# Attention, ELU and tanhshrink layers on one core: how the first pairs of heads are prepared, placed and scheduled, and the transpose of the last 64 keys

## Chip, cores and metric

The kernel runs on one core of a Trainium2 chip. The metric is the device time of one execution in microseconds (us). Engines are PE (TensorE; its weight loads are listed apart as PEld), DVE (VectorE), ACT (ScalarE), POOL (GpSimd) and SP (SyncE, which here only issues DMAs).

## What is computed

An attention with rotary position encoding over 4 batches x 8 heads, 576 positions, head size 64, all in float32; then two dense layers over the 2304 tokens. The change touches the attention alone. Cut to what matters:

```python
def _attn_ref(q, k, v):                       # (4, 8, 576, 64)
    def rotate(x):
        x1, x2 = x[..., :half], x[..., half:]
        return np.concatenate([x1 * cos - x2 * sin, x1 * sin + x2 * cos], axis=-1)
    q_rot, k_rot = rotate(q), rotate(k)
    scores = scale * np.matmul(q_rot, k_rot.transpose(0, 1, 3, 2))
    scores = scores - np.max(scores, axis=-1, keepdims=True)
    attn = np.exp(scores)
    attn = attn / (np.sum(attn, axis=-1, keepdims=True) + 1e-09)
    return np.matmul(attn, v)

def reference(...):
    x = attn_out.transpose(0, 2, 1, 3).reshape(2304, 512)
    x = elu(x @ moe_w_in) @ moe_w_out
    h = x @ moe2_w_in
    return (h - np.tanh(h)) @ moe2_w_out
```

## The kernel before

The 32 heads are worked in 16 pairs. A pair has nine items: four blocks of 128 queries (u = 0 to 3) for each of its two heads (h = 0, 1), and one item (u = 4, h = None) with the last 64 queries of both heads. So there are 144 items, and one loop over i runs them in an order written out by hand. In step i it emits, in this order: the loads that are due, the row maximum of item i on DVE (L224), the scores of item i+1 on PE (L215), the exponentials of item i on ACT (L238), the copies of the last step's transposes out of PSUM (L269 on DVE, L271 on ACT), the normalising of item i-1 on POOL (L255, with a sum and a reciprocal on DVE, L251 and L252), the preparation steps that are due, one part of a weight conversion, the transposes of item i-4 on PE (L295 and, for the last 64 keys, L308 or L301), and the products with v that are due on PE (L329). Each engine works its own instructions strictly in this order. Scores lie in two PSUM buffers, so the scores of item i+2 wait for the exponentials of item i.

**Preparation.** Before a pair can be scored, q and k of both heads (x = 0 and x = 1 in `prep`) pass five steps: multiply with the cosine table (step 0) and the sine table (step 1), add (step 2), round to a high part on ACT (step 3, L155), and take the low part on DVE (step 4, L160). Then `place` copies high and low parts by DMA to where the matmuls want them: four DMAs of 288 KB for k (L182) and four of 144 KB for q (L185). These read 64 partitions and write 64; the loads from memory (L130, L359, L361) write all 128. The first two items are scored directly from the sums of step 2 (L197), without the parts. For pair 1 the table `early` gives the step i at which each of the five is emitted: before the change (0, 0, 1, 2, 3) for q and (0, 0, 0, 1, 2) for k; its loads are issued right behind those of pair 0. The multiplications of step 0 of later pairs run on POOL, step 1 on DVE for pairs 0 and 1 and on POOL from pair 2 on.

**Weight conversion.** In the attention, eight blocks of the dense layers' weights are also converted (`conv_w`), each in five parts spread over every second step: part 0 on ACT (L74), part 1 two DVE instructions (L76, L77), parts 2 and 3 one each (L81, L85), part 4 ACT and POOL (L91, L92). With c = 9*(p%2) + r - 3 they fall, for an even pair, on the steps r = 3, 5, 7 of its nine and on r = 0 and 2 of the next pair.

**Last 64 keys.** Each transposed block of probabilities has 128 keys; 576 leaves 64. For the blocks u = 0 to 3 one 128x128 transpose serves both heads (L308). For u = 4 two 64x64 matmuls with the identity do it (L301), and the copy out is 128x64. The last product with v reads 64 rows of the one head and 64 rows of zeros.

## Time and profile before

| | |
|---|---|
| median of 3 runs | 1100.6 us (1100.6 to 1100.99) |
| the profiled execution | 1101.16 us, its span 1099.0 us |
| PE busy in the span | 1060.1 us (96%) |
| PEld, DVE, ACT, POOL busy | 960.0, 756.5, 724.3, 697.6 us |
| attention, up to the last product with v | about 311 us |
| first items, up to the transposes of item 8 | 45.6 us |
| first matmul of the kernel | 12.46 us, when the second sum of pair 0 is ready (12.41 us) |
| pair 1 on DVE | its additions done at 19.15 us, its low parts at 26.6 us |
| PE without work before item 8 | 32.3 to 34.1 us; its granted clock then 0.50, from 34.7 to 38.1 us |

The span runs from the first to the last instruction of the trace; the profiled execution's own time is 2.16 us longer. A busy PE is not a PE at its peak, so the table says only that PE is seldom without work, and where it is not.

### The profile page before, as it was taken

What the parts mean: (1) busy time and instruction counts of PE and PEld (TensorE: products, weight loads), DVE (VectorE), ACT (ScalarE), POOL (GpSimd) and SP (SyncE); (2) the same over time, 40 slices, a digit from 0 to 9 for tenths busy, and PEclk for the clock granted to TensorE, in tenths of its full rate; (3) what the DMA queues carried; (4) which work ended last, traced back from release to release, by engine and by line L of the source; (5) the groups of instructions that cost most, each with busy time, mean ns of one, the idle gap of its engine ahead of it and who ended that gap; (6) DMA issues with size and microseconds to landing.
All of it is one profiled execution on the core that took longest, in us unless ns stands there. A gap on an engine that the chain in (4) does not pass through costs nothing.

```text
span 1099.0 us, 18847 instructions
## 1 busy us (share of the span) xinstructions
PE 1060.1 (96%) x6512; PEld 960.0 (87%) x6512; DVE 756.5 (69%) x1435; ACT 724.3 (66%) x1562; POOL 697.6 (63%) x652
## 2 busy tenths in 40 slices
PE   2999999999999999999999999999999999999998
PEld 1777777777889999999999999988998999888986
DVE  6888889888745564675776765376767667766674
ACT  2676767777757666565555555488777877878672
POOL 3888888888558856555455565566566655755552
PEclk9999999999999999999999999999999999999999
DMA  7777676867214444354443673255445754456431
GB/s 232 215 214 190 187 199 200 215 186 206 74 45 139 125 157 141 101 178 152 127 144 128 225 240 117 94 211 194 167 158 197 252 205 163 181 163 231 169 127 58
DMA packets 85950, 184.27 MB, mean 168 GB/s; under 512 B 10592, under 2 KB 46432, under 8 KB 85856
## 3 DMA queue, kind: packets, MB, share of 16 engines
q1 hardware_dynamic: 78080, 154.76, 44.4%
q10 hardware_dynamic: 7776, 28.32, 8.8%
q8 instruction: 52, 0.85, 0.3%
q14 instruction: 42, 0.34, 0.1%
HBM read 126.94 MB, written 27.79 MB: 141 GB/s over the span
## 4 chain that ended last, share of the span: by engine, by line
PE 79%; DVE 9%; POOL 4%; ACT 3%; issue 2%; DMA 2%; SPq 0%; ACTq 0%; POOLq 0%; DVEq 0%
PE y L511 18%; PE h L454 18%; PE yb L705 14%; PE hb L740 9%; PE o L329 7%; PE s L215 6%; PE pt L295 4%; PE cvb L740 3%; DVE nm L224 2%; DVE fn L773 1%; DMA v<-in_v 1%; POOL blk L495 1%; DVE aT L269 1%; DVE t L152 1%; POOL blk L612 1%
## 5 line engine op out<-in xcount | busy, mean ns | idle before, releaser
L255 POOL TENSOR_SCALAR a<-a,r 128x576 f32<-128x576 f32 x144 | 137.0, 963 | 56.9 <-DVE r L252 37.7
L495 POOL TENSOR_TENSOR gt<-fn,gt 128x384 fp32r<-128x384 f32 x119 | 123.3, 1036 | 76.7 <-ACT gt L494 69.1
L238 ACT ACTIVATE a<-s,nm 128x576 f32<-128x576 f32 x144 | 107.2, 744 | 85.7 <-DVE nm L224 71.6
L705 PE MATMUL yb<-wb,blk 128*128 128x512 f32 x603 | 154.3, 392 | 0.4 <-POOL blk L495 0.4
L740 PE MATMUL hb<-blk,wa 128*128 128x384 f32 x720 | 139.8, 337 | 2.0 <-DVE fn L773 2.0
L740 PEld LDWEIGHTS hb<-blk,wa 128*128 128x128 f32 x720 | 127.0, 188 | 7.3 <-DVE fn L773 3.0
L705 PEld LDWEIGHTS yb<-wb,blk 128*128 128x128 f32 x603 | 112.5, 188 | 22.7 <-POOL blk L495 0.8
L462 ACT ACTIVATE fn<-h 128x384 f32<-128x384 f32 x96 | 47.3, 492 | 125.1 <-PE h L454 105.7
L224 DVE TENSOR_REDUCE nm<-s 128x1 f32<-128x576 f32 x144 | 107.8, 752 | 30.1 <-PE s L215 28.2
L495 POOL TENSOR_TENSOR blk<-fn,blk 128x384 fp32r<-128x384 f32 x67 | 71.3, 1064 | 87.9 <-ACT blk L494 59.4
L454 PE MATMUL h<-blk,wa 128*128 128x384 f32 x576 | 107.9, 335 | 0.8 <-POOL blk L55 0.6
L511 PE MATMUL y<-gt,wa 128*128 128x384 f32 x576 | 107.7, 334 | 0.1
L454 PE MATMUL h<-blk,wb 128*128 128x384 f32 x576 | 107.6, 334 | 0.0
L511 PE MATMUL y<-gt,wb 128*128 128x384 f32 x576 | 107.6, 334 | 0.0
L479 DVE TENSOR_SCALAR cvb<-fm 128x512 f32<-128x512 f32 x56 | 38.9, 694 | 98.9 <-ACT fm L477 96.3
L454 PEld LDWEIGHTS h<-blk,wa 128*128 128x128 f32 x576 | 100.3, 188 | 1.8 <-POOL blk L55 0.9
L511 PEld LDWEIGHTS y<-gt,wa 128*128 128x128 f32 x576 | 100.5, 188 | 0.4 <-issue 0.4
L511 PEld LDWEIGHTS y<-gt,wb 128*128 128x128 f32 x576 | 100.6, 188 | 0.0
L454 PEld LDWEIGHTS h<-blk,wb 128*128 128x128 f32 x576 | 100.5, 188 | 0.0
L92 POOL TENSOR_TENSOR fm<-fm,fn 128x512 fp32r<-128x512 f32 (+1 forms) x48 | 58.3, 1219 | 57.0 <-ACT fn L91 55.8
L150 POOL TENSOR_TENSOR t<-t,tabs 128x576 f32<-128x576 f32 x59 | 86.1, 1460 | 6.4 <-DMA t<-in_qk 6.3
L329 PE MATMUL o<-aT,v 128*64 128x256 f32 (+1 forms) x768 | 88.2, 336 | 1.9 <-ACT aT L271 1.8
(128 smaller groups left out, 2289.2 us busy)
## 6 DMA issues: line engine op xcount, KB each, us to landing
wa<-wi SPq DMA_DIRECT2D x96, 448.0 KB, 4.9
wb<-wo SPq DMA_DIRECT2D x48, 512.0 KB, 5.9
k<-hl SPq DMA_DIRECT2D x64, 288.0 KB, 4.7
t<-in_qk SPq DMA_DIRECT2D x30, 576.0 KB, 5.1
fm<-in_w2o ACTq DMA_DIRECT2D x16, 512.0 KB, 3.8
fm<-in_w2i ACTq DMA_DIRECT2D x14, 512.0 KB, 3.6
fm<-in_w1i ACTq DMA_DIRECT2D x12, 512.0 KB, 3.7
wi<-fn SPq DMA_DIRECT2D x24, 256.0 KB, 2.0
```

Source lines behind the costliest of these rows:

```text
L92: nc.gpsimd.tensor_tensor(out=lo, in0=f, in1=hi.bitcast(F32), op=ALU.subtract)
L150: eng.tensor_tensor(out=t[:, i, :], in0=t[:, i, :], in1=tabs[:, i, :], op=ALU.mult)
L215: nc.tensor.matmul(out=s[:, half, o0:o0 + n], lhsT=w, rhs=k[:, part, c0:c0 + n], start=(m == 0 and part == 0), stop=(m == len(terms) - 1 a ...
L224: nc.vector.tensor_reduce(out=nm, in_=s_t[i][:, :, 0:288], axis=AX.XY, op=ALU.max, negate=True)
L238: nc.scalar.activation(out=a.rearrange("p (x c) -> p x c", x=2), in_=s[:, :, 0:288], func=AF.Exp, bias=nm_t.pop(i), scale=1.0, accum_out=den,)
L255: nc.gpsimd.tensor_scalar(out=a, in0=a, scalar1=r[:, x:x + 1], scalar2=1.0, op0=ALU.mult, op1=ALU.mult)
L329: nc.tensor.matmul(out=o[sl, 0:n], lhsT=w, rhs=m, start=(c == 0), stop=(c == 4))
L454: nc.tensor.matmul(out=hp, lhsT=w[:, wp, ws], rhs=x_hl(t, xp, c), start=(m == 0), stop=(m == 3 * KC - 1))
L495: nc.gpsimd.tensor_tensor(out=g[:, 1, :], in0=f, in1=g[:, 0, :].bitcast(F32), op=ALU.subtract)
L511: nc.tensor.matmul(out=y_t[e][:, 0:NB], lhsT=w[:, wp, es], rhs=gt[:, gp, :], start=st, stop=sp)
L705: nc.tensor.matmul(out=y, lhsT=gt[:, gp, es], rhs=w[:, wp, :], start=(j == 0 and k == 0), stop=(j == NJ - 1 and k == 2))
L740: nc.tensor.matmul(out=bank, lhsT=w[:, wp, o:o + 128], rhs=x[:, xp, cc, :], start=(start and k == 0), stop=(stop and k == 5), skip_group_c ...
```

## The change

- **Loads at the start:** k, table, q, and again k, table, q; the loads of pair 1 and of v come behind the placing of pair 0.
- **Matmuls on zeros:** DVE clears 512 columns of `xa`, and PE multiplies them by themselves six times ahead of the first scores and three times after those of item 1.
- **Preparation of pair 0:** all on DVE, k before q; step 0 writes its product to a PSUM buffer of the scores (`prod`), step 1 writes in place, step 2 adds. q is scaled in steps 0 and 1.
- **Placing pair 0:** head 0's DMAs are issued by SP, head 1's by ACT.
- **Pair 1 later:** its five steps are emitted at i = 0, 3, 4, 4, 5 for q and for k.
- **Weight conversion:** c = 9*(p%2) + r - 9, so the parts fall on r = 0, 2, 4, 6, 8 of every odd pair, six steps later than before.
- **Last 64 keys:** one 128x128 transpose of the keys 448 to 575 of both heads in place of the two 64x64 matmuls; the copy out is 128x128; v gets 64 more columns and one more DMA of 16 KB per pair (64 rows).

```diff
@@ -122,7 +122,7 @@
         qa_t = [acst.tile([128, 640], F32R, name=f"qa{i}") for i in range(2)]
         qb_t = [acst.tile([128, 640], F32R, name=f"qb{i}") for i in range(2)]
 
-        vt_t = [acst.tile([128, 640], F32, name=f"v{i}") for i in range(2)]
+        vt_t = [acst.tile([128, 704], F32, name=f"v{i}") for i in range(2)]
         t_t, hl_t, v_t, k_t = {}, {}, {}, {}
 
         def load_qk(p, x):
@@ -136,24 +136,31 @@
             for h in range(2):
                 sl = slice(64 * h, 64 * h + 64)
                 nc.sync.dma_start(out=t[sl, 512 + 64 * h:576 + 64 * h], in_=v[p, sl, 512:576])
+            nc.sync.dma_start(out=t[64:128, 640:704], in_=v[p, 0:64, 512:576])
 
         def prep(p, x, i):
             t = t_t[p, x]
-            mul = SCALE if p > 0 and x == 0 else 1.0
-            if i < 2:
-                if p == 0 and x == 0:
-                    nc.vector.scalar_tensor_tensor(
-                        out=t[:, i, :], in0=t[:, i, :], scalar=SCALE, in1=tabs[:, i, :], op0=ALU.mult, op1=ALU.mult
-                    )
+            mul = SCALE if x == 0 else 1.0
+            if p == 0 and i < 3:
+                o, a, b = (z.rearrange("p (x c) -> p x c", x=2) for z in (t[:, i % 2, :], t[:, i % 2, :], tabs[:, i % 2, :]))
+                if i == 0:
+                    o = prod[x] = ps_s.tile([128, 2, 512], F32, tag="s", name="prod")[:, :, 0:288]
+                if i < 2:
+                    nc.vector.scalar_tensor_tensor(out=o, in0=a, scalar=mul, in1=b, op0=ALU.mult, op1=ALU.mult)
                 else:
-                    eng = nc.vector if p < 2 and i == 1 else nc.gpsimd
-                    eng.tensor_tensor(out=t[:, i, :], in0=t[:, i, :], in1=tabs[:, i, :], op=ALU.mult)
+                    b = t[:, 1, :].rearrange("p (x c) -> p x c", x=2)
+                    nc.vector.tensor_tensor(out=o, in0=prod[x], in1=b, op=ALU.add)
+            elif i < 2:
+                eng = nc.vector if p == 1 and i == 1 else nc.gpsimd
+                eng.tensor_tensor(out=t[:, i, :], in0=t[:, i, :], in1=tabs[:, i, :], op=ALU.mult)
             elif i == 2:
                 nc.vector.tensor_tensor(out=t[:, 0, :], in0=t[:, 0, :], in1=t[:, 1, :], op=ALU.add)
             elif i == 3:
+                mul = mul if p else 1.0
                 hl_t[p, x] = p1.tile([128, 2, S], F32R, tag=f"hl{x}", name=f"hl{x}")
                 nc.scalar.mul(hl_t[p, x][:, 0, :], t[:, 0, :], mul)
             else:
+                mul = mul if p else 1.0
                 hl = hl_t.pop((p, x))
                 if p > 0:
                     t_t.pop((p, x))
@@ -161,28 +168,23 @@
                     out=hl[:, 1, :], in0=t[:, 0, :], scalar=mul, in1=hl[:, 0, :].bitcast(F32),
                     op0=ALU.mult, op1=ALU.subtract,
                 )
-                if p == 0 and x == 0:
-                    first_hl.append(hl)
                 for h in range(2):
-                    if p > 0:
-                        place(p, x, h, hl)
-                    elif x == 1:
-                        place(p, 0, h, first_hl[0])
-                        place(p, 1, h, hl)
-
-        first_hl = []
+                    place(p, x, h, hl)
+
+        prod = {}
 
         def place(p, x, h, hl):
             src = hl[64 * h:64 * h + 64].bitcast(F32)
+            eng = nc.scalar if p == 0 and h == 1 else nc.sync
             if x == 1:
                 k_t[p, h] = p2.tile([128, 2, S], F32R, tag=f"k{h}", name=f"k{h}")
             for part in range(2):
                 ps = slice(64 * part, 64 * part + 64)
                 if x == 1:
-                    nc.sync.dma_start(out=k_t[p, h][ps].bitcast(F32), in_=src)
+                    eng.dma_start(out=k_t[p, h][ps].bitcast(F32), in_=src)
                 else:
                     qt, c0 = ((qa_t, 0), (qb_t, 64))[h]
-                    nc.sync.dma_start(out=qt[p % 2][ps, c0:c0 + S].bitcast(F32), in_=src[:, part, :])
+                    eng.dma_start(out=qt[p % 2][ps, c0:c0 + S].bitcast(F32), in_=src[:, part, :])
 
         items = [(p, u, h) for p in range(NPAIR) for u in range(5) for h in ((0, 1) if u < 4 else (None,))]
         s_t, a_t, n_t, aT_t, nm_t = {}, {}, {}, {}, {}
@@ -286,7 +288,7 @@
                                     p2.tile([128, 256], F32, tag="aTr", name="aTr"))
                 else:
                     aT_t[p, grp] = (p1.tile([128, 2, 4, 64], F32, tag="aT2", name="aT2"),
-                                    p1.tile([128, 64], F32, tag="aTr2", name="aTr2"))
+                                    p1.tile([128, 128], F32, tag="aTr2", name="aTr2"))
             aT, aTr = aT_t[p, grp]
             q0 = 128 * (u % 2)
             pt = ps_t.tile([128, 4, 128], F32, tag="pt", name="pt")
@@ -296,11 +298,8 @@
             if h is None:
                 evac(aT, pt.rearrange("p c (h q) -> p h c q", h=2))
                 pr = ps_t.tile([128, 4, 128], F32, tag="pt", name="pr")
-                for hh in range(2):
-                    sl = slice(64 * hh, 64 * hh + 64)
-                    nc.tensor.matmul(out=pr[sl, 0, 0:64], lhsT=a[sl, 0, 512:576], rhs=ident[sl, sl],
-                                     start=True, stop=True)
-                evac(aTr[:, 0:64], pr[:, 0, 0:64])
+                nc.tensor.transpose(pr[:, 0, :], a[:, 0, 448:576], ident)
+                evac(aTr, pr[:, 0, :])
                 return
             evac(aT[:, h, :, q0:q0 + 128], pt)
             if h == 1:
@@ -324,8 +323,10 @@
                 sl = slice(64 * h, 64 * h + 64)
                 if c < 4:
                     w, m = vt[:, 128 * c + 64 * h:128 * c + 64 * h + 64], aT[:, h, c, 0:n]
+                elif grp < 2:
+                    w, m = vt[:, 512 + 64 * h:576 + 64 * h], aTr
                 else:
-                    w, m = vt[:, 512 + 64 * h:576 + 64 * h], aTr[:, 0:n]
+                    w, m = vt[:, 640 - 64 * h:704 - 64 * h], aTr[:, 64 * h:64 * h + 64]
                 nc.tensor.matmul(out=o[sl, 0:n], lhsT=w, rhs=m, start=(c == 0), stop=(c == 4))
             if c < 4:
                 return
@@ -340,7 +341,7 @@
         NI = 9
         first_w = [(0, kind, c) for c in range(NJ) for kind in range(2)]
         sched = {}
-        early = {1: ((None, 0, 0, 1, 2, 3), (None, 0, 0, 0, 1, 2)), 2: ((0, 4, 5, 7, 7, 8), (4, 7, 9, 11, 12, 13))}
+        early = {1: ((None, 0, 3, 4, 4, 5), (None, 0, 3, 4, 4, 5)), 2: ((0, 4, 5, 7, 7, 8), (4, 7, 9, 11, 12, 13))}
         for p in range(1, NPAIR):
             i0 = NI * (p - 1)
             for x in range(2):
@@ -354,33 +355,40 @@
             sched.setdefault(i0 + 7, []).append((load_v, p))
         with tc.manual_schedule():
             for x in range(2):
-                t = t_t[0, x] = p2.tile([128, 2, S], F32, tag=f"t{x}", name=f"t{x}")
-                for i in range(2):
-                    nc.sync.dma_start(out=t[:, i, :], in_=qk[0, :, 2 * x + i, :])
-                    if x == 0:
-                        nc.sync.dma_start(out=tabs[:, i, :], in_=tab[:, i, :])
-            load_qk(1, 0)
-            load_qk(1, 1)
-            load_v(0)
+                t_t[0, x] = p2.tile([128, 2, S], F32, tag=f"t{x}", name=f"t{x}")
+            for i in range(2):
+                nc.sync.dma_start(out=t_t[0, 1][:, i, :], in_=qk[0, :, 2 + i, :])
+                nc.sync.dma_start(out=tabs[:, i, :], in_=tab[:, i, :])
+                nc.sync.dma_start(out=t_t[0, 0][:, i, :], in_=qk[0, :, i, :])
+            nc.vector.memset(xa[:, 0:512], 0.0)
+            nc.vector.memset(zero, 0.0)
             make_identity(nc, ident)
-            nc.vector.memset(zero, 0.0)
+
+            def warm(k):
+                w = ps_t.tile([128, 512], F32, tag="pt", name="warm")
+                for _ in range(k):
+                    nc.tensor.matmul(out=w, lhsT=xa[:, 0:128], rhs=xa[:, 0:512], start=True, stop=True)
+
+            warm(6)
             for i in range(2):
                 nc.scalar.copy(out=qa_t[i][:, S:640], in_=zero)
                 nc.scalar.copy(out=qb_t[i][:, 0:64], in_=zero)
                 nc.gpsimd.memset(vt_t[i][64:128, 512:576], 0.0)
-                nc.gpsimd.memset(vt_t[i][0:64, 576:640], 0.0)
-            for i in range(3):
-                prep(0, 0, i)
+                nc.gpsimd.memset(vt_t[i][0:64, 576:704], 0.0)
             for i in range(3):
                 prep(0, 1, i)
+                prep(0, 0, i)
             n = len(items)
             pend = []
             nw = list(range(len(first_w)))[::-1]
             emit_s(0)
             PV_AT = ((1, 1, 1, 3, 3), (1, 1, 1, 3, 3), (2, 2, 2, 2, 2))
             for i in range(3, 5):
-                for x in range(2):
+                for x in (1, 0):
                     prep(0, x, i)
+            load_qk(1, 1)
+            load_qk(1, 0)
+            load_v(0)
             for i in range(n + D + 1):
                 p, r = divmod(i, NI)
                 for f, *arg in sched.get(i, ()):
@@ -392,6 +400,8 @@
                     emit_max(i)
                 if i + 1 < n:
                     emit_s(i + 1)
+                if i == 0:
+                    warm(3)
                 if i < n:
                     emit_exp(i)
                 flush()
@@ -401,7 +411,7 @@
                     for f, *arg in sched.get(i, ()):
                         if f is prep:
                             f(*arg)
-                    c = NI * (p % 2) + r - 3
+                    c = NI * (p % 2) + r - NI
                     if c >= 0 and c % 2 == 0 and c // 2 < NCV and p // 2 < len(first_w):
                         key = first_w[p // 2]
                         conv_w(key, c // 2, 512 * (p // 2 % 3))
```

## Rows read from the trace of the kernel before

**Rows 1.** Busy time by stage: stretch, length, engines with counts, PEclk, DMA share, GB/s
```profile
45.61:311.60 265.99, 259.57 (x2221) 205.37 (x2221) 221.97 (x507) 185.53 (x469) 212.51 (x197) 1.00 0.67 178
```
**Rows 2.** Chain of work that ended last, 17 to 48 us: start, us, what
```profile
19.13 4.44 DMA k<-hl
...
29.73 1.21 DVE fm L76
...
30.96 1.53 DVE fm L77
```
**Rows 3.** PE, timeline 19 to 46 us: start, us, instruction, [idle before <-releaser]
```profile
19.86 1.30 PE L215 MATMUL s<-k,qa 128*128 128x288 f32 x4 [5.10 <-DMA k<-hl]
23.81 1.30 PE L215 MATMUL s<-k,qb 128*128 128x288 f32 x4 [2.65 <-DMA k<-hl]
...
37.03 1.25 PE L215 MATMUL s<-k,qa 128*128 128x288 f32 x4
...
40.10 0.81 PE L215 MATMUL s<-k,qb 128*128 128x288 f32 x4
```
**Rows 4.** DMA issues at 2.59 to 3.1, at 4.06 and at 14.98 us: size, us to landing
```profile
t<-in_qk SPq DMA_DIRECT2D x2, 288.0 KB, 5.3
...
t<-in_qk SPq DMA_DIRECT2D x1, 576.0 KB, 7.8
...
k<-hl SPq DMA_DIRECT2D x1, 288.0 KB, 3.1
```
**Rows 5.** As rows 1, single microseconds: loads at 8, placing at 21, a lower clock at 35
```profile
8.00:9.00 1.00, 0.00 (x0) 0.00 (x0) 1.00 (x2) 0.31 (x1) 1.00 (x1) 1.00 1.02 408
...
21.00:22.00 1.00, 0.16 (x1) 0.00 (x0) 0.80 (x3) 0.00 (x0) 0.00 (x0) 1.00 1.05 221
...
35.00:36.00 1.00, 1.00 (x7) 1.00 (x5) 0.80 (x2) 1.00 (x4) 1.00 (x1) 0.50 0.97 390
```
**Rows 6.** POOL and DVE, timeline 7 to 20 us: multiplications with the tables
```profile
7.92 5.75 POOL L150 TENSOR_TENSOR t<-t,tabs 128x576 f32<-128x576 f32 x3 [5.86 <-DMA t<-in_qk]
...
8.58 1.96 DVE L150 TENSOR_TENSOR t<-t,tabs 128x576 f32<-128x576 f32 x1
...
15.54 1.41 DVE L150 TENSOR_TENSOR t<-t,tabs 128x576 f32<-128x576 f32 x2
```
**Rows 7.** Groups by shape, 45 to 300 us: busy, mean ns | idle before
```profile
L224 DVE TENSOR_REDUCE nm<-s 128x1 f32<-128x576 f32 x130 | 97.3, 752 | 25.7 <-PE s L215 23.8
...
L160 DVE SCALAR_TENSOR_TENSOR hl<-t,hl 128x576 fp32r<-128x576 f32 x27 | 28.6, 1061 | 4.7 <-ACT hl L155 4.0
...
L152 DVE TENSOR_TENSOR t<-t 128x576 f32<-128x576 f32 x26 | 23.4, 901 | 2.6 <-POOL t L150 2.6
```
**Rows 8.** Chain of work at 97 us; PE's timeline behind two of the L301
```profile
97.35 0.11 PE pr L308
...
98.43 0.26 PE pr L301 x4
...
98.62 1.52 PE L329 MATMUL o<-aT,v 128*64 128x256 f32 x12
...
116.31 2.11 PE L329 MATMUL o<-aT,v 128*64 128x256 f32 x12
```
**Rows 9.** As rows 1, from one L301 to the next; DVE is the third busy time
```profile
45.61:62.88 17.27, 17.25 (x148) 13.62 (x147) 14.82 (x34) 11.49 (x31) 15.42 (x15) 1.00 0.75 201
62.88:81.29 18.41, 17.04 (x148) 13.62 (x147) 17.07 (x40) 14.06 (x37) 14.73 (x14) 1.00 0.75 198
81.29:98.36 17.07, 17.01 (x147) 13.58 (x147) 13.77 (x30) 11.59 (x29) 14.96 (x15) 1.00 0.75 207
...
240.22:258.62 18.40, 17.08 (x147) 13.62 (x146) 17.05 (x40) 14.04 (x37) 15.07 (x14) 1.00 0.77 212
258.62:275.72 17.10, 17.04 (x147) 13.62 (x147) 13.77 (x30) 11.59 (x29) 14.46 (x14) 1.00 0.64 156
```
**Rows 10.** Waits of SP's queue, 45 to 300 us: us in total, times, longest
```profile
SPq L182 <- DVE hl L160: 84.3, 14, 6.8
```

## The prediction, as it stood before the changed kernel ran

> **What bounds the kernel now.** I read the busy time by stage first: from 45.6 us to the end of the attention PE is busy 259.57 of 265.99 us [rows 1], and the dense layers behind it are not touched. So a gain has to come from the first 45.6 us, which the attention then carries to the end, or from PE's or DVE's share of each pair. The chain of waits comes second, for the first stage: it runs through the DMA that places k of pair 0 (until 23.57 us), then through the first weight conversion on DVE (29.7 to 32.5 us), and only then along PE [rows 2]. PE's timeline says the same: the scores of item 2 wait for k until 19.86 us, those of item 3 until 23.81 us; from item 9 (37.03 us) and item 10 (40.10 us) on, pair 1, PE has its order to work off [rows 3]. The views by single microseconds come third: the DMA engines are full while the parts are placed, at 221 GB/s with a share of 1.05, while the loads from memory ran at 408 GB/s with a share of 1.02 [rows 5]. So the first stage is one of DMA volume. The time between the transposes of item 8 of one pair and of the next comes last, for what a pair costs [rows 9].
>
> **The change, part by part.**
>
> *Start of pair 0.* The six loads keep their places in SP's queue; the fifth and sixth, issued at 2.59 and about 3.05 us, land 5.3 us later [rows 4], at 7.9 and 8.4 us. DVE then has a multiplication, a second one, and two additions, 0.76 us each as its instructions took there without POOL (1.41 us for two [rows 6]): the second sum is ready at about 10.9 us in place of 12.4. The memset of `xa` and the matmuls on zeros lie in the idle time ahead (PE does nothing before 12.46 us); the three behind item 1 are over long before item 2 can start. I give them no gain: the granted clock was 0.50 at 35 us, 1.2 of 2.4 GHz [rows 5], after PE had stood still from 32.3 to 34.1 us, and here the pauses, from about 7 to 11 us and again until item 2, are longer. If they do hold the clock, they save about 0.5 us per item (1.30 us at 20 us, 0.81 at 40 [rows 3]) for two or three items that wait for DMA anyway.
>
> *Placing pair 0.* High and low parts of k are ready at about 11.7 us. One k DMA lands 3.1 us after its issue [rows 4], of which 1.3 us is 288 KB at 221 GB/s; data flow from about 13.5 us. All eight DMAs are 1.77 MB: 8.0 us at 221 GB/s, so 21.5 us. Before, the last landed at 23.57 us, but item 2's came first and let it start at 19.86. With two queues side by side, both heads land together: item 2 at 21.5 (1.6 us later), item 3 at 22.8 (1.0 us earlier). That two queues move more in the same time no row of before shows; the ends are 221 and 408 GB/s [rows 5]. I take 221, because the share is full already there.
>
> The Trainium skill has a rule against this part: "SBUF — State Buffer", section "Can I just issue two DMAs to hit both halves?", says no, all DMAs run on the same 16 engines, and two at once on the two halves of the partitions gained 6%. By that the eight DMAs take 7.5 us, and the sum below is 0.5 us lower. No stretch of this trace has two queues placing, so it can't be checked before.
>
> *Pair 1 later.* This is where I expect the loss. Its loads, issued at 3.5 to 4.5 us, had landed by 11.9 us (4.06 + 7.8 [rows 4]), and DVE multiplied and added in its idle time from 15.5 us. Now these 1.18 MB queue behind the placing: 2.9 us at 408 GB/s, so they land at about 24.5 us. What is queued behind them: POOL's two multiplications, and behind these the normalising of item 1, which the first transposes need; on DVE the two multiplications stand ahead of the maximum of item 4. DVE and POOL now multiply side by side, as they did from 8 to 13 us, where one took DVE 1.96 us and POOL needed 5.75 us for three; without POOL it was 0.7 us [rows 6]. From item 3's maximum at 24.2 us, DVE's order is: maximum 0.75, two multiplications 3.8, maximum 0.75, sums 0.4, two additions 1.8, maximum 0.75, a copy 0.7, the two low parts 2.1 [rows 7], which ends at about 35.2 us; before, the low parts were done at 26.6. SP then issues four q DMAs and k in turn, 0.5 to 0.6 us each; the second k DMA of head 0 is issued at about 36.5 and lands at about 40.2 us. Item 9 starts there, 3.2 us later than before [rows 3], and item 10 behind its transposes and products at 42.8 us, 2.7 us later. From then on PE works the same order as before. Bounds: with 408 GB/s in the placing all this is 3.6 us earlier, -0.9; if PE, idle before item 9, meets the lower clock then, 1.5 us more, +4.2. I take **+2.7 us**.
>
> *Weight conversion six steps later.* The first one leaves the start: its 2.8 us on the chain [rows 2] are not in the order above. But it now falls into the full pairs. Seven stretches without a conversion, of which the first, second and last stand in [rows 9], have a mean of 17.34 us; the first six with one (first and last shown) 18.13 us. So one more of these costs **+0.8 us**; the last lies in a pair that prepares nothing any more, as before. DVE is busy 3.3 us more in such a stretch, of which 0.8 us shows, a quarter. In the new place the DVE parts (r = 2, 4, 6) meet additions and low parts, which fall on the same r; in the old place (r = 5, 7, 0) they met none of them. The five steps around hold one addition more, 0.90 us [rows 7]. With a quarter of it, seven times: **+1.5 us**. Bounds: all of it, +6.3; or, as the parts no longer meet POOL's multiplications at r = 3, 5, 7, 0, all of the 0.8 us hidden, -5.5.
>
> *Transpose of the last 64 keys.* In the chain L301 has 0.26 us per pair and the 128x128 transpose 0.11 [rows 8], so PE is free 0.15 to 0.16 us earlier. In nine of the first fifteen pairs the products behind it run through at once in 1.52 us; in the others they stand 0.5 to 0.6 us for a copy (2.11 us [rows 8]), and the time is lost there. So 9 x 0.16 = **-1.5 us**; bounds -2.4 (all fifteen) and 0. The copy of 128 columns in place of 64 costs well under 0.1 us, on engines that then wait. The extra 16 KB DMA of v costs SP one issue, about 0.6 us a pair, under the 6 us that SP waits in each pair for the low part (84.3 us in 14 times [rows 10]).
>
> *Sum.* 2.7 + 0.8 + 1.5 - 1.5 = +3.5 us on the profiled execution's 1101.16 us: 1104.7. That execution is 0.56 us above the median of the runs, so 1104.1 us is to be compared with 1100.6.
>
> **The rivals.** *Faster:* the two queues move the two halves side by side at about 400 GB/s. Then pair 0 is placed by 18 us, pair 1 loaded by 21, item 10 starts at 39.2 us (-0.9), the transposes show in full (-2.4), the conversions keep their price (+0.8): 1098.1 us, and a little lower if they are hidden in their new place. It decides at one point: the last DMA of pair 0 has landed at 18 us, not at 21. For it: the two heads' DMAs read different halves. Against it: the share of 1.05 [rows 5]. *Same:* the six loads land a microsecond sooner with nothing behind them, and the multiplications of pair 1 meet POOL only once (1.2 us less): start +0.5, conversions +0.8, transposes -1.5, so 1100.4 us. *Much slower:* the bunched DVE parts stall PE for their whole 0.90 us each time, +6.3 in place of +1.5: 1108.9 us. For it: DVE is busy 17.07 of 18.41 us in such a stretch [rows 9]; against it: only a quarter of 3.3 us shows today. *The zeros don't hold the clock*: this is already in the sum, at no price.
>
> **How the numbers follow.** Forecast (1102.6 to 1106.2, by itself) 0.43, much slower 0.15, same 0.17, faster 0.25. From the same cases: slower by over 0.2% (2.2 us, about what a measurement of this kernel can tell from no change) 0.58, within it 0.17, faster 0.25. The likeliest is the forecast, 1104.1 us; the range goes from the faster rival with part of the conversions hidden, 1096.5, to the slower one, 1109.0.
>
> **What would show it.** Item 2's scores near 21.5 us and item 3's right behind; the second multiplication of pair 1 on DVE near 25 us with about 1.9 us; item 9's scores waiting for k, near 40 us, and L301's place (the transpose of item 8) near 48 us in place of 45.61. If item 9 starts before 37 us, the start is a gain and the sum is wrong there. Stretches with a conversion of more than 18.1 us on average show its new place as a loss, shorter ones refute it. If the products behind the new transpose run in 1.52 us as often as before, its 0.16 us is gained in those pairs only.

## The result, and the profile of the changed kernel

| | before | after |
|---|---|---|
| median, us | 1100.8 (1100.6 to 1101.3) | 1112.4 (1109.6 to 1114.4) |
| ratio, with 95% interval | 1 | 1.0103 (1.0075 to 1.0130) |
| profiled execution / its span, us | 1101.16 / 1099.0 | 1114.15 / 1112.3 |
| first L301 (last 64 keys of item 8), us | 45.61 | 49.42 |
| from there, 15 stretches to the last L301, us | 262.25 | 271.68 |
| from the last L301 to the end, us | 791.2 | 791.2 |

The change makes the kernel 11.6 us slower; the forecast was 3.5 us slower, with 1109.0 as the upper end of the range. The last three rows of the table are of the profiled executions, and that of the changed kernel is one of its two longer ones. Between the two lie 13.2 us of span: 3.8 at the start, 9.4 in the 15 stretches of full pairs, nothing behind them. So the start came out near its forecast, and the full pairs did not.

PE's timeline of the changed kernel at the start, the rows that answer to [rows 3] (start, us, instruction, idle before and what ended it):

```profile
21.07 1.30 PE L217 MATMUL s<-k,qa 128*128 128x288 f32 x4 [5.13 <-DMA qa<-hl]
22.17 1.16 PE L217 MATMUL s<-k,qb 128*128 128x288 f32 x4
...
35.78 1.33 PE L217 MATMUL s<-k,qa 128*128 128x288 f32 x4 [2.65 <-ACT a L240]
...
39.23 1.30 PE L217 MATMUL s<-k,qa 128*128 128x288 f32 x4
43.10 0.81 PE L217 MATMUL s<-k,qb 128*128 128x288 f32 x4
...
49.42 0.33 PE L301 MATMUL pr<-ident,a 128*128 128x128 f32 x1 [0.74 <-DVE aT L271]
```

Items 2 and 3 start at 21.07 and 22.17 us, items 9 and 10 at 39.23 and 43.10: item 10 is 3.0 us later than before. L301 is late by another 0.8 us, 0.74 of them a wait for a copy. What is ahead of that copy stands in the chain of waits of the same stretch (as [rows 2]):

```profile
15.11 5.72 DMA qa<-hl
...
24.14 3.54 DVE t L155 x2
...
31.57 2.55 DVE hl L167 x2
...
46.20 0.76 DVE t L157
46.96 0.35 DVE fm L76
...
47.33 0.77 DVE fm L77
48.11 0.66 DVE nm L226
48.77 0.60 DVE aT L271
```

The two multiplications of pair 1 and its two low parts are on the chain, as the forecast had it; and the first weight conversion (`fm`) is on it again, at 47 us in place of 30.

From one L301 to the next (as [rows 9]: stretch, length, busy time of PE, PEld, DVE, ACT, POOL, granted clock, DMA share, GB/s):

```profile
49.42:67.11 17.69, 17.15 (x143) 13.64 (x144) 15.36 (x36) 11.68 (x32) 15.90 (x15) 1.00 0.76 204
67.11:86.23 19.12, 17.18 (x146) 13.48 (x144) 15.63 (x38) 13.30 (x36) 14.94 (x14) 1.00 0.73 198
86.23:104.87 18.64, 18.58 (x143) 14.24 (x144) 13.76 (x32) 12.15 (x30) 15.26 (x14) 0.91 0.68 178
```

Two things are new. The second stretch takes 19.12 us where it took 18.41. And in three of the 15 stretches the granted clock is 0.91; in the kernel before it was 1.00 in every full pair. Single microseconds around the first of these, as [rows 5]:

```profile
85.00:86.00 1.00, 0.00 (x0) 0.00 (x0) 1.00 (x2) 1.00 (x3) 1.00 (x1) 1.00 1.06 425
...
87.00:88.00 1.00, 1.00 (x8) 0.62 (x6) 1.00 (x2) 0.80 (x3) 1.00 (x2) 0.50 0.00 0
```

PE stands still for all of the microsecond from 85 us, waiting at L301; from 86.4 to 89.8 us the clock is at 0.50, 1.2 of 2.4 GHz. A stretch with such a drop is 1.55 us longer than the same stretch without (18.64 against 17.08 us in the kernel with the conversion alone moved, below). So the 9.4 us are three drops, 4.7 us, and 4.8 us of longer stretches. The drops do not seem to be the same in every execution: the two at 1114 us have a mean granted clock of 0.984 and 0.985, the two at 1110 us 0.990 and 0.991. The new start alone, whose profiled execution has no drop in its pairs, has 0.989 to 0.991 (below), and 1114.15 less 4.7 is 1109.5 us, about where the two shorter executions lie. By this estimate they have no drop, and the drops are why this kernel's runs spread over 4.8 us where those of the kernel before beside them spread over 0.7. So the median lies between two groups of two.

### The profile page after: what moved, and what is told of

It reads as the page before. It is cut to its first block, busy times and chain, and to the rows that moved or that the text cites. A ratio compares the mean times of both kernels' runs of the same rounds, so it can differ in the third digit from the quotient of the medians.

```text
span 1112.3 us, 18783 instructions
## 1 busy us (share of the span) xinstructions
PE 1075.3 (97%) x6482; PEld 967.0 (87%) x6482; DVE 747.9 (67%) x1437; ACT 724.7 (65%) x1562; POOL 700.2 (63%) x651
## 4 chain that ended last, share of the span: by engine, by line
PE 77%; DVE 10%; POOL 4%; ACT 4%; issue 2%; DMA 2%; SPq 1%; ACTq 0%; DVEq 0%; POOLq 0%
PE y L521 18%; PE h L464 17%; PE yb L715 14%; PE hb L750 8%; PE o L330 6%; PE s L217 6%; PE cvb L750 3%; PE pt L297 3%; DVE nm L226 2%; DVE fn L783 1%; DVE t L157 1%; ACT a L240 1%; DMA k<-hl 1%; POOL blk L622 1%; DVE aT L271 1%
## 5 line engine op out<-in xcount | busy, mean ns | idle before, releaser
L257 POOL TENSOR_SCALAR a<-a,r 128x576 f32<-128x576 f32 x144 | 143.2, 1005 | 50.5 <-DVE r L254 34.0
L155 POOL TENSOR_TENSOR t<-t,tabs 128x576 f32<-128x576 f32 x58 | 83.3, 1438 | 21.6 <-DMA t<-in_qk 21.6
L330 PE MATMUL o<-aT,v 128*64 128x256 f32 (+1 forms) x768 | 91.1, 342 | 1.6 <-ACT aT L273 1.4
L92 POOL TENSOR_TENSOR fm<-fm,fn 128x512 fp32r<-128x512 f32 (+1 forms) x48 | 58.3, 1219 | 54.3 <-ACT fn L91 53.1
```

Source lines behind the costliest of these rows:

```text
L92: nc.gpsimd.tensor_tensor(out=lo, in0=f, in1=hi.bitcast(F32), op=ALU.subtract)
L155: eng.tensor_tensor(out=t[:, i, :], in0=t[:, i, :], in1=tabs[:, i, :], op=ALU.mult)
L257: nc.gpsimd.tensor_scalar(out=a, in0=a, scalar1=r[:, x:x + 1], scalar2=1.0, op0=ALU.mult, op1=ALU.mult)
L330: nc.tensor.matmul(out=o[sl, 0:n], lhsT=w, rhs=m, start=(c == 0), stop=(c == 4))
```

## The experiments

Every run was timed against the kernel before on the same chip (1100.6 to 1101.1 us). S is the new start, C the conversion moved, T the full transpose. "L301" is the start of the first L301, "pairs" the 15 stretches behind it; both are of the one profiled execution, the median is of all.

| kernel | median, us | ratio, 95% interval | L301 | pairs |
|---|---|---|---|---|
| before | 1100.8 | | 45.61 | 262.25 |
| S alone | 1105.7 | 1.0042 (1.0027 to 1.0057) | 50.34 | 263.9 |
| C alone | 1107.5 | 1.0057 (1.0042 to 1.0072) | 45.46 | 268.5 |
| T alone | 1101.1 | 0.9999 (0.9989 to 1.0008) | 44.45 | 262.8 |
| C and T | 1108.4 | 1.0060 (1.0043 to 1.0077) | 45.77 | 271.0 |
| S, pair 1 early | 1100.7 | 0.9998 (0.9988 to 1.0007) | 44.94 | 262.3 |
| S, one queue | 1106.0 | 1.0045 (1.0028 to 1.0062) | 51.20 | 262.1 |
| S, no zeros | 1105.5 | 1.0043 (1.0027 to 1.0058) | 49.78 | 262.3 |
| C, five steps | 1109.2 | 1.0073 (1.0058 to 1.0088) | 45.73 | 270.1 |
| C, part 1 a step later | 1105.8 | 1.0043 (1.0026 to 1.0060) | 44.73 | 268.2 |
| C, 64 columns on DVE | 1100.9 | 0.9999 (0.9989 to 1.0008) | 45.84 | 262.7 |
| before, 64 columns on DVE | 1097.3 | 0.9966 (0.9953 to 0.9979) | 44.13 | 259.7 |
| C, last transpose in the output's bank | 1107.8 | 1.0064 (1.0049 to 1.0079) | 43.41 | 270.8 |
| before, the same | 1103.4 | 1.0020 (1.0010 to 1.0029) | 44.97 | 264.4 |
| S, pair 1 early, last transpose in the output's bank | 1102.8 | 1.0018 (1.0008 to 1.0027) | 44.79 | 264.3 |
| before, conversion where DVE idles | 1098.6 | 0.9975 (0.9966 to 0.9985) | 44.68 | 260.2 |
| after, conversion where DVE idles | 1102.7 | 1.0020 (1.0010 to 1.0029) | 48.77 | 260.4 |
| S, pair 1 early, conversion where DVE idles | 1098.1 | 0.9973 (0.9963 to 0.9984) | 44.06 | 260.2 |
| the same with T | 1098.5 | 0.9977 (0.9968 to 0.9986) | 44.15 | 260.3 |

### The three parts alone

**S.** All of the start, the conversion at `r - 3` and the two 64x64 matmuls kept.

> The kernel before with the new start alone (loads, zeros, pair 0 on DVE, two queues, pair 1 later); conversion and transpose as before. Theory: the first L301 starts 3 to 4 us later than 45.6 us, and this is carried to the end; with the first conversion back in the start, another 1 to 3 us: 1104 to 1107 us. Rival (the start itself is a gain and the first stage pays only for what else was changed): 1100 us or less.

**C.** One line of the kernel before:

```diff
-                    c = NI * (p % 2) + r - 3
+                    c = NI * (p % 2) + r - NI
```

> The kernel before with the weight conversion alone moved six steps later. Theory (the conversion's DVE parts now meet additions and low parts and stall PE): the stretches from L301 to L301 add up to several us more than before, 1104 to 1108 us in all, the first stage a little shorter (by up to 2.8 us up to the first L301). Rival (the conversion's place is as good, the transpose does it): 1099 to 1101 us.

**T.** The hunks of the diff on `vt_t` and its memset, `load_v`, `emit_t` and `emit_pv` alone.

> The kernel before with the full transpose for the last 64 keys alone (and its DMA of v). Theory (a small gain): 1098 to 1100 us, no lower granted clock behind 45 us. Rival (the transpose keeps PE waiting or lets the clock fall, where the matmuls with the identity did not): 1103 us or more, with stretches of granted clock 0.50 behind 45 us.

**C and T.**

> The kernel before with the moved conversion and the full transpose, start as before. Theory (the two act on their own and add up): c_only's difference plus t_only's, 1103 to 1107 us. Rival (only together they make PE pause long enough for a lower clock): well above that sum, 1108 us or more.

Measured: +4.7, +6.5, +0.1 us, and +7.4 for C and T together; the three single edits add up to 11.3 of the 11.6 us. That they add up so well is partly luck. In the profiled executions the start costs 4.7 us by itself and 3.8 in the whole change, and the pairs 6.2 us with C alone and 9.4 in the whole change, where three drops of the clock stand against one. But each part keeps its sign, and each term of the sum can be looked at by itself. That the start alone is later at L301 (50.34 us) than the whole change (49.42) fits its first conversion, which is still in the start. The 1.6 us more in its pairs are of this execution, at 1107.3 us the longest of its four.

### The start: is it the later pair 1?

S with the loads of pair 1 and of v issued where they were, and its steps as before:

```diff
-        early = {1: ((None, 0, 3, 4, 4, 5), (None, 0, 3, 4, 4, 5)), ...
+        early = {1: ((None, 0, 0, 1, 2, 3), (None, 0, 0, 0, 1, 2)), ...
...
                 nc.sync.dma_start(out=t_t[0, 0][:, i, :], in_=qk[0, :, i, :])
+            load_qk(1, 0)
+            load_qk(1, 1)
+            load_v(0)
...
-            load_qk(1, 1)
-            load_qk(1, 0)
-            load_v(0)
             for i in range(n + D + 1):
```

> The kernel before with the new start of pair 0 alone (order of the loads, matmuls on zeros, products in PSUM, parts placed by two queues), but the loads of pair 1 and of v right behind the six first loads and the steps of pair 1 where they were before. Theory 'pair 1 later': the start of the change loses because pair 1 is loaded and prepared later; then all of the 4.7 us is gone, the first transpose of item 8 is at 45.0 to 46.0 us and the time 1100 to 1101.5 us. Rival 'placing': it loses because item 2 starts at 21.7 us in place of 19.9 and the parts of both heads land together; then 2 to 4 us stay, 1103 to 1105 us.

PE's timeline of this kernel:

```profile
21.51 1.14 PE L216 MATMUL s<-k,qa 128*128 128x288 f32 x4 [5.19 <-ACT hl L160]
...
38.54 0.80 PE L216 MATMUL s<-k,qb 128*128 128x288 f32 x4
...
44.94 0.33 PE L302 MATMUL pr<-ident,a 64*64 64x64 f32 x4 [0.83 <-DVE aT L270]
```

Item 2 is as late as in the changed kernel (21.51 against 19.86 us before), and still item 10 starts at 38.54 us, 1.6 us earlier than before, and all of the 4.7 us is gone. So the loss of the start is pair 1's, and with pair 1 early the later item 2 costs nothing. The edit moves the loads of pair 1 and its steps together; which of them weighs more it does not show.

**One queue, and no zeros.** S with `eng = nc.sync` in `place`, and S without `warm(6)` and `warm(3)`:

> The kernel before with the new start of pair 0 (conversion and transpose in the old form), all parts of pair 0 placed by SP's queue instead of two queues. It stands beside the run with the new start and two queues (1105.7 us, item 2 at 21.71 us). If two queues move no more than one, as the rate of 221 GB/s at a full share said, the last part lands at the same time within 1 us and the time is 1105 to 1107 us; item 2 may start earlier, near 20 us, because its head comes first. If two queues help, item 3 is 2 us or more later, 1107 to 1109 us.

> The kernel before with the new start of pair 0 (conversion and transpose in the old form), without the matmuls on zeros. With them it took 1105.7 us. The forecast gave them nothing: 1105 to 1106.5 us. If they hold the clock for what follows, the scores of items 0 to 4 run at the lower clock without them and it is 0.5 to 1.5 us slower, 1106.2 to 1107.2 us.

The end of the placing, in the chain of waits with two queues, and in the list of issues at 18.05 us with one (size, us to landing):

```profile
15.89 5.57 DMA qa<-hl
```

```profile
qb<-hl SPq DMA_DIRECT2D x1, 144.0 KB, 2.6
```

With two queues the first of the eight DMAs is issued at 11.80 us and the last lands at 21.46, 9.7 us; with one it is 11.15 to 20.68, 9.5 us. So two queues do not place the parts in less time, and the 400 GB/s of the rival "faster" are not there. With one queue the parts of head 0 come first, items 2 and 3 start 1.9 us earlier (19.86 and 20.95 against 21.71 and 22.81 us), and the kernel takes the same time within its intervals, so the place of these two items does not decide. The rule of the Trainium skill, "SBUF — State Buffer", section "Can I just issue two DMAs to hit both halves?" (6% from a second transfer on the other half), is borne out in kind; even the 6% do not show over the whole placing. The zeros make no difference in time either. They do what they are put there for, as the eight matmuls of the first two items show, without them (2.30 us) and with them (1.25 us, S with one queue):

```profile
10.43 2.30 PE L198 MATMUL s<-t,t 64*128 64x288 f32 x8 [10.43 <-DVE t L151]
```

```profile
10.34 1.25 PE L198 MATMUL s<-t,t 64*128 64x288 f32 x8 [0.65 <-DVE t L151]
```

That microsecond ends in the wait for the placed parts.

### The conversion: first two explanations, which fell

**Meeting additions.** The forecast's own mechanism: the DVE parts (r = 2, 4, 6) fall on the steps of additions and low parts. One step earlier they fall on r = 1, 3, 5 and meet none:

```diff
-                    c = NI * (p % 2) + r - 3
+                    c = NI * (p % 2) + r - 8
```

> The kernel before, with the weight conversion five steps later instead of six. Its absolute value on ACT falls on step r = 8 of an even pair, its DVE parts on r = 1, 3, 5 of an odd pair, its split into two parts (ACT, POOL) on r = 7; the additions and low parts of the next pairs fall on r = 2, 4, 6, 8. Theory 'meeting': the change loses because the DVE parts of the conversion fall on the same steps as an addition or a low part. Then this kernel, which comes one step earlier and meets none of them, has only the price of one more conversion in full pairs (0.8 us): 1101 to 1103 us, stretches with a conversion near 18.1 us on average. Rival 'ends': it loses because the first and last part (ACT and POOL) lie at the boundary between two pairs. Then one step hardly matters: 1105 to 1108 us. Rival 'clock': it loses by stretches of granted clock 0.50 that the pauses of PE bring; then the time goes with the number of these, 1.5 us each.

It is slower still, 1109.2 us, with a granted clock of 1.00 throughout its full pairs. So neither meeting nor the clock is the cause here; where there are drops, they come on top.

**Less work on DVE.** The conversion's DVE instructions on 64 of 512 columns (the other 448 are left unconverted), in the new place and in the old:

> The kernel before, with the conversion six steps later, and the DVE instructions of the conversions done in the attention on 64 of their 512 columns (the other columns of these eight weight blocks are left unconverted, ACT's and POOL's parts are as they were). To be read against the next run, the same with the conversion in its old place. 'Meeting': without the DVE work nothing is left to meet, so both take the same time within 2 us, near 1095 us. 'Ends': the new place still loses 4 to 6 us against the old one. 'Clock': as many drops of the granted clock behind 42 us as with full DVE work, and 1.5 us for each.

> The kernel before, conversion in its old place, with the DVE instructions of the conversions done in the attention on 64 of their 512 columns (the other columns of these eight weight blocks are left unconverted). It gives the price of the DVE parts in the old place. By the stretches of the kernel before, 18.1 against 17.3 us, seven times 0.8 us and the 2.8 us of the first one on the chain at the start: 1093 to 1096 us. If the stretches with a conversion are longer for ACT's or POOL's parts, it stays at 1099 to 1101 us.

Between the two places 3.6 us stay, which none of the three cases had, and the old place is slower than its forecast of 1093 to 1096 us. That seemed to speak for ACT and POOL, but the DVE instructions had not become nothing. DVE at the step in question, new place, 64 columns:

```profile
78.89 0.19 DVE L77 TENSOR_SCALAR fm<-fm 128x64 f32<-128x64 f32 x1
79.12 0.55 DVE L78 TENSOR_SCALAR fm<-fm 128x64 uint32<-128x64 uint32 x1
```

0.69 us from the start of the one to the maximum behind the other, where 512 columns take 1.15 (next fences). The test took away less than half of the suspect.

**POOL's share.** ACT and POOL are not cleared by that, and the traces show a share of POOL. In the new place the split of the conversion (part 4, L92 on POOL) falls on r = 8, ahead of a multiplication for the next pair (L150). In pairs 8 and 10 the addition on DVE then waits for that product. Pair 8 with C alone:

```profile
164.72 1.28 POOL L92 TENSOR_TENSOR wa<-fm,wa 128x512 fp32r<-128x512 f32 x1
...
166.69 1.41 POOL L150 TENSOR_TENSOR t<-t,tabs 128x576 f32<-128x576 f32 x1
...
168.13 1.30 DVE L152 TENSOR_TENSOR t<-t 128x576 f32<-128x576 f32 x1 [0.51 <-POOL t L150]
169.36 0.74 DVE L224 TENSOR_REDUCE nm<-s 128x1 f32<-128x576 f32 x1
```

and before:

```profile
167.98 0.76 DVE L152 TENSOR_TENSOR t<-t 128x576 f32<-128x576 f32 x1
```

From the maximum of r = 2 to that of r = 3 it is 3.40 and 3.45 us in these two pairs with C alone, 3.42 and 3.48 with 64 columns, 3.20 and 3.46 in the changed kernel, and 2.26 and 2.27 us before. That is 2.3 us with C alone, 2.4 with 64 columns and 2.1 in the changed kernel, and no DVE part of a conversion falls there. It is not made good later: pair 10 takes 17.86 us with C alone and 16.67 in the run with part 1 a step later (below), which has no such wait, and but for these 1.2 us its steps agree within 0.15 us. No run moves the split by itself, so this share is read from the traces and not tested.

**The fourth PSUM buffer.** L301 is where PE's wait shows: with C alone it waits 10.6 us in nine of its 16 places, before 3.5 us in three. It needs a fourth transpose buffer of three and so waits for the copy of item 7's transposes. At 78 to 82 us, before:

```profile
78.47 0.75 DVE L152 TENSOR_TENSOR t<-t 128x576 f32<-128x576 f32 x1
79.14 1.41 DVE L224 TENSOR_REDUCE nm<-s 128x1 f32<-128x576 f32 x2
79.93 0.74 ACT L238 ACTIVATE a<-s,nm 128x576 f32<-128x576 f32 x1 [0.58 <-DVE nm L224]
80.66 0.58 ACT L271 COPY aT<-pt 128x512 f32<-128x512 f32 x1
81.29 0.33 PE L301 MATMUL pr<-ident,a 64*64 64x64 f32 x4 [1.32 <-ACT aT L271]
```

and with C alone:

```profile
78.28 0.76 DVE L152 TENSOR_TENSOR t<-t 128x576 f32<-128x576 f32 x1
78.95 0.42 DVE L76 TENSOR_SCALAR fm<-fm 128x512 f32<-128x512 f32 x1
79.40 0.78 DVE L77 TENSOR_SCALAR fm<-fm 128x512 uint32<-128x512 uint32 x1
80.10 1.40 DVE L224 TENSOR_REDUCE nm<-s 128x1 f32<-128x576 f32 x2
80.88 0.74 ACT L238 ACTIVATE a<-s,nm 128x576 f32<-128x576 f32 x1 [2.19 <-DVE nm L224]
81.61 0.57 ACT L271 COPY aT<-pt 128x512 f32<-128x512 f32 x1
82.23 0.33 PE L301 MATMUL pr<-ident,a 64*64 64x64 f32 x4 [1.94 <-ACT aT L271]
```

The chain is plain: addition, conversion, maximum, exponential, copy, L301, each released by the one ahead. Two ways to cut it: part 1 (L76 and L77) a step later, behind that copy (`c in (0, 3, 4, 6, 8)`), or L301's output into 64 free columns of the output's bank, so that it needs no buffer.

> The kernel with the conversion alone moved six steps later, but its second part (the two DVE instructions of lines 74 and 77) one step later still, on r = 3 in place of r = 2. Theory 'ring': the loss sits in one place, the transpose of the last 64 keys (L301), which needs a fourth PSUM buffer out of three and waits for the copy of item 7's transposes; on r = 2 the conversion stands ahead of the maximum, the exponential and so of that copy. In the kernel with the conversion moved L301 waited 10.6 us in the 15 stretches, in the kernel before 3.5. On r = 3 the conversion stands behind that copy: L301 waits 3 to 5 us again and the time is 1100.5 to 1103 us. Rival 'bunching': DVE has as much to do in the same steps, so the loss stays, 1105.5 to 1108 us.

> The kernel with the conversion alone moved six steps later, and the transpose of the last 64 keys written into free columns (320 to 383) of the output's PSUM bank instead of a fourth buffer of the ring of three. What is computed is the same. 'Ring': L301 has nothing to wait for, and of the 10.6 us that it waited in this placing at least 5 are gone, the others return as waits of the products for the same copies: 1098 to 1103 us, and the difference to the next run is under 2.5 us. Rival 'bunching': PE waits for the same copies a step later, in the products; the loss of 6 us against the next run stays.

> The kernel before, conversion in its old place, with the transpose of the last 64 keys written into free columns (320 to 383) of the output's PSUM bank, as the control of the run ahead. 'Ring': the 3.5 us that L301 waits in three of the 15 stretches are gone in part: 1097.5 to 1100.5 us. 'Bunching': nothing changes, 1100 to 1101.5 us.

Both missed. With part 1 a step later, L301's waits are down to the 2.5 us of three stretches, and the time is still 1105.8 us: PE's weight loads for the scores now wait 11.5 us for the exponentials, before 3.5. With L301 in the output's bank 4.5 us of the 6.5 stay, and the edit has a price of its own (the copy of L301's output waits 9.2 us for the products in that bank, in the control as well, and the control is 2.3 us slower than before, which neither of its cases had), so nothing finer can be read from it. That bank together with the early pair 1 gave 1102.8 us, above both of its cases:

> The new start of pair 0 with pair 1 loaded and prepared early as in the kernel before, the old place of the conversion, and the transpose of the last 64 keys in free columns of the output's PSUM bank. If the two edits add up, it is 0.4 us under the run ahead (the start alone, with pair 1 early, gave 1100.7 us), 1097 to 1100 us; if the wait only moves, 1100 to 1101.5 us.

L301 is where the loss shows, not where it comes from: cut there, it comes out elsewhere. What stays the same in all of them is a conversion on DVE ahead of a maximum.

### The conversion: DVE's idle time, step by step

DVE works in order, so a part emitted in step r delays the maximum of step r + 1, unless DVE would have waited for the scores there anyway. Worked out from DVE's timeline, 13 pairs of each kernel (2 to 14): DVE's mean idle time ahead of the maximum of step r, and the mean time from that maximum to the next, in us. The even pairs of C alone have no DVE part of a conversion on their steps:

| step r | 0 | 1 | 2 | 3 | 4 | 5 | 6 | 7 | 8 | pair |
|---|---|---|---|---|---|---|---|---|---|---|
| no conversion: idle ahead of it | 0.00 | 0.99 | 0.11 | 0.17 | 0.04 | 0.64 | 0.15 | 0.80 | 0.68 | 3.6 |
| no conversion: to the next maximum | 2.24 | 1.13 | 2.51 | 1.07 | 3.18 | 1.05 | 2.79 | 1.60 | 2.08 | 17.65 |
| C: parts on 2, 4, 6 (odd pairs) | 1.98 | 1.17 | **3.11** | 0.93 | **3.73** | 1.07 | 2.89 | 1.54 | 2.09 | 18.52 |
| before: parts on 5, 7 (even pairs) | 2.27 | 1.13 | 2.18 | 1.13 | 3.13 | **2.25** | **2.03** | 1.56 | 2.21 | 17.88 |
| before: part on 0 (odd pairs) | **2.19** | 1.10 | 2.18 | 0.99 | 3.47 | 1.04 | 2.93 | 1.40 | 2.12 | 17.43 |

Two of the idle times as they stand in DVE's timeline of C alone (r = 5 and 8 of one pair):

```profile
101.86 0.76 DVE L224 TENSOR_REDUCE nm<-s 128x1 f32<-128x576 f32 x1 [0.69 <-PE s L215]
...
107.31 0.76 DVE L224 TENSOR_REDUCE nm<-s 128x1 f32<-128x576 f32 x1 [0.85 <-PE s L215]
```

The first two rows, even pairs of C alone, hold pairs 8 and 10 with their wait for POOL: without these two, step 2 has 2.14 us in place of 2.51. Even and odd pairs differ besides (step 4), so C's odd pairs are best held against the odd pairs of before, the last row.

Ahead of the maximum of r = 3 there is 0.17 us, of r = 4 0.04. Part 1 on r = 2 takes 1.15 us; its step is 3.11 us where the kernel before has 2.18, 0.93 more, which is close to its time less the idle time. Part 2 on r = 4 takes 0.7 us and has 0.64 of idle time ahead of the next maximum: that step is 0.26 us longer than before, and 0.27 is what the one drop of the clock, in pair 13, adds to the mean of six pairs. In the old place part 1 fell on r = 5: that step grows by 1.2 us, but the next shrinks by 0.8, and idle time follows on r = 7 and 8. In the run five steps later part 1 is on r = 1 (idle ahead of 2: 0.11) and that step has 2.36 in place of 1.17 us; with part 1 a step later it is on r = 3 and that step has 2.67 in place of 1.0. So in all three losing places part 1 stands ahead of a maximum without idle time. The size of the three losses (6.5, 8.1 and 4.7 us) does not follow from the table alone.

For C alone the 6.2 us of its pairs can be taken apart: 1.6 are the drop, 2.3 the two waits for POOL, and the other 2.3, as the remainder, the DVE parts in their new place less what they cost in the old one. The 9.4 us of the changed kernel come apart in the same way into 4.7, 2.1 and 2.6.

To test it, the parts went where idle time follows, in the kernel before, in the changed kernel and with the early pair 1. ACT's part and POOL's split move with them, both to r = 5:

```diff
-                    c = NI * (p % 2) + r - 3
-                    if c >= 0 and c % 2 == 0 and c // 2 < NCV and p // 2 < len(first_w):
+                    k = {5: 0, 6: 1, 9: 2, 13: 3, 14: 4}.get(NI * (p % 2) + r)
+                    if k is not None and p // 2 < len(first_w):
                         key = first_w[p // 2]
-                        conv_w(key, c // 2, 512 * (p // 2 % 3))
+                        conv_w(key, k, 512 * (p // 2 % 3))
```

> The kernel before with the conversion at other steps of the two pairs: absolute value on r = 5, the two DVE instructions of the second part on r = 6 of the even pair, the third part on r = 0 and the fourth on r = 4 of the odd pair, the split on r = 5. Theory 'slack': a DVE part costs what it delays the next maximum, that is its time less the time for which DVE stands idle ahead of the following maxima. In pairs without a conversion DVE waits for the scores ahead of the maximum of r = 1, 5, 7 and 8 (about 1.0, 0.6, 0.8 and 0.7 us) and hardly ahead of r = 2, 3, 4 and 6 (0.04 to 0.17 us). Here each part (1.1, 0.7, 0.7 us) falls in front of one of the idle times, so the conversions are nearly hidden: two pairs take 34.9 to 35.1 us in place of 35.3, the time is 1097.5 to 1100 us. Rival 'distance': what counts is that the conversion is later than in the kernel before, or that its parts meet additions (r = 6) and low parts (r = 4): 1102 to 1107 us.

> The changed kernel, with the conversion at the steps of the run ahead (r = 5, 6 of the even pair, 0, 4, 5 of the odd one). 'Slack': the 6.5 us that the new place of the conversion costs are gone, and what stays against the kernel before is the later pair 1, 4 to 5 us, less what the hidden conversions give: 1101.5 to 1106 us, without a drop of the granted clock in the full pairs. 'Distance': 1108 to 1113 us.

> The new start of pair 0 with pair 1 loaded and prepared early as in the kernel before, old transpose, and the conversion at the steps of the two runs ahead. If both hold, it is 0.4 us under the first run of this group, 1097 to 1099.6 us, faster than the kernel before and the changed one. 'Distance': 1102 to 1107 us.

All three came out as written: 1098.6, 1102.7 and 1098.1 us. Two pairs take 34.95 us (17.40 and 17.55 from maximum to maximum) against 35.31 before and 36.17 with C alone. In the changed kernel the place of the conversion alone is worth 9.7 us, and no stretch of its full pairs has a granted clock under 1.00. Pairs 8 and 10 do not wait for POOL there either (2.26 and 2.27 us), so these runs show what the place is worth, not how DVE's parts and POOL's split share in it. DVE's timeline with part 1 on r = 6, of the pair shown last:

```profile
103.63 0.42 DVE L76 TENSOR_SCALAR fm<-fm 128x512 f32<-128x512 f32 x1
104.08 0.78 DVE L77 TENSOR_SCALAR fm<-fm 128x512 uint32<-128x512 uint32 x1
104.79 0.74 DVE L224 TENSOR_REDUCE nm<-s 128x1 f32<-128x576 f32 x1
105.84 0.76 DVE L224 TENSOR_REDUCE nm<-s 128x1 f32<-128x576 f32 x1 [0.32 <-PE s L215]
```

The maximum of r = 7 follows at once, and ahead of the next one DVE still waits 0.32 us: the delay has ended there. The third kernel is faster than both the kernel before and the changed one.

### The transpose once more

> The best run so far (new start with pair 1 early, conversion where DVE is idle, 1098.1 us) with the full transpose of the last 64 keys in addition. The forecast gave the transpose -1.5 us (0.15 us in the nine pairs whose products run through at once). The reading of the run with the transpose alone is that the 0.15 us show only in pairs whose products then wait for a copy, and not in the others, where the transpose itself starts later. If that is right, nothing changes: 1097.6 to 1098.7 us. If it was hidden by the waits that the conversion caused, it is gained now: 1096 to 1097 us.

1098.5 against 1098.1 us: nothing, with the waits of the conversion out of the way as well.

## Why the forecast was wrong, point by point

By its terms, in the profiled execution: the start came to +3.8 us where +2.7 were forecast, the full pairs to +9.4, where the conversion was forecast at +2.3 and the transpose at -1.5.

- **First sums and parts of pair 0: right, within 0.7 us.** The second sum is ready at 10.2 us (forecast 10.9), the parts of k at 11.1 (11.7).
- **Placing: right.** Items 2 and 3 at 21.07 and 22.17 us (forecast 21.5 and 22.8), and the last DMA lands at 20.83 us, near the 21 that the forecast set against the rival's 18. The price of 221 GB/s, nearer than 408, held: 216 to 244 in the three windows of 2 us from 13 to 19 us.
- **Pair 1 later: right in cause and size.** Low parts done at 34.1 us (35.2), item 9 at 39.23 (40.2), item 10 at 43.10 (42.8): +3.0 us for +2.7. Only the link was another one. The forecast let item 9 wait for the DMA of k; in fact item 8 waits 2.65 us for an exponential, whose maximum stood on DVE behind the two low parts. With pair 1 early all of it is gone.
- **The first conversion leaves the start: wrong in what it gives.** The forecast took its 2.8 us off the chain. C alone shows 0.15 us (L301 at 45.46). Items 8 and 9 come 2.3 and 3.2 us earlier, then the next thing is late, an addition of pair 2 on DVE. POOL, which had waited for the load, was done with the product for it at 41.62 us; by its row the addition was held until 41.81 by a DMA of pair 1's q:

```profile
36.68 1.41 POOL L150 TENSOR_TENSOR t<-t,tabs 128x576 f32<-128x576 f32 x1 [2.73 <-DMA t<-in_qk]
...
40.22 1.40 POOL L150 TENSOR_TENSOR t<-t,tabs 128x576 f32<-128x576 f32 x1
...
41.81 1.19 DVE L152 TENSOR_TENSOR t<-t 128x576 f32<-128x576 f32 x1 [0.34 <-DMA qb<-hl]
```

  Behind that addition the conversion stands on the chain again, at 43 us, and in the changed kernel at 47, where L301 is 0.8 us later than item 10 was.
- **The conversion's new place: the term that failed, +2.3 us where 6.5 were measured** (C alone). The step that failed is that the new place was priced by its DVE parts alone. ACT's and POOL's parts were put at nothing without a reason, though the split on r = 8 stands ahead of a multiplication for the next pair, and so was what longer waits do to PE. In their place the traces show 2.3 us behind POOL's split and 1.6 us of a drop of the clock with C alone, 2.1 and 4.7 us in the changed kernel.
- **"A quarter": near in size, wrong as a rule.** What is left for the DVE parts, 2.3 us with C alone and 2.6 in the changed kernel, is as much as forecast, by luck. The share of DVE's added time that showed in the old place was taken for the new one, with a surcharge for additions met. That share is no property of the work: five steps later, where no addition is met, the loss is 8.1 us without a drop, and where DVE idles it is a gain. It depends on the idle time ahead of the next maxima, and that is 2.6 us on the steps behind the old parts (r = 6, 7, 8 and 1) and 0.17 behind the first part in its new place. The trace of before would have given it: DVE's idle time ahead of the maximum by step is 0.0 to 0.3 us there on r = 2, 3 and 4 in even and odd pairs alike. The rival "much slower" had about the size of the whole term (7.1 us), and a wrong mechanism, since the parts needn't meet anything.
- **DVE's busy time pointed the wrong way.** The forecast's lower bound rested on the parts no longer running beside POOL's multiplications, and they don't. In groups by shape the four DVE instructions of a conversion take 2.60 us with C alone and 3.05 before. Over the 15 stretches (columns as in [rows 1]), before and C alone:

```profile
45.61:307.86 262.25, 255.83 (x2175) 202.07 (x2174) 221.00 (x503) 184.87 (x466) 212.51 (x197) 1.00 0.67 181
```

```profile
45.46:313.95 268.49, 256.57 (x2173) 202.64 (x2173) 212.80 (x505) 184.60 (x467) 216.19 (x196) 0.99 0.66 175
```

  DVE is busy 8.2 us less, and the stretches are 6.2 us longer. The Trainium skill, "SBUF — State Buffer", section "Who interferes with whom", says that DVE and GpSimd share a pair of ports, and that of two instructions that both want it the one issued first keeps the other out for its whole length. The shorter instructions agree with it (the first of the four takes 0.42 us with C alone and 0.87 before), and the longer time shows that it wasn't what decides here.
- **Drops of the granted clock: not in the forecast at all.** They follow PE's waits of 1.9 us at L301 in the changed kernel, 1.55 us each, 4.7 us in the profiled execution. The second of the three waits is that of pair 8, behind POOL's split. They are a consequence: with the conversion moved away there are none.
- **The transpose: -1.5 us forecast, 0 measured.** The forecast had the gain in the wrong pairs. Transposes and products of two pairs, T alone:

```profile
61.40 0.60 PE L296 MATMUL pt<-ident,a 128*128 128x128 f32 x4
...
62.04 2.14 PE L329 MATMUL o<-aT,v 128*64 128x256 f32 x12
...
96.91 0.60 PE L296 MATMUL pt<-ident,a 128*128 128x128 f32 x4
...
97.69 1.52 PE L329 MATMUL o<-aT,v 128*64 128x256 f32 x12
```

  Before, the products start 0.79 us behind the transposes in both pairs (62.35 to 63.14, 97.83 to 98.62 us). Now it is 0.64 in the first and 0.78 in the second. The 0.15 us is there only in the six pairs like the first, whose products then stand still for a copy (2.14 us, before 1.99), and is lost in that. In pairs like the second the weights of the transpose wait for a PSUM buffer, and it takes as long as the two matmuls did. The extra DMA cost nothing, as forecast.
- **Two queues, zeros: right,** no gain in time from either.

## What to carry to other kernels

Work added to an engine that runs in order costs its time less the idle time ahead of the next instruction that others wait for; make a table of that idle time by step of the loop, from the trace of before, and put the work in front of the idle steps. Busy shares, and the share that the same work costs in another place, don't give that price. Do it for every engine that gets a part of the work: here a part on POOL, ahead of a product that DVE needs, cost about as much as the parts on DVE. A wait that grows is where a delay shows; cut it there and the delay comes out at the next wait, so follow the chain back to the instruction that is late with nothing to wait for.
